# Attention into a token mixer on one core: p read once in fp32, all first scores by 32-row pieces, a new order

## The chip, the cores and the metric

The kernel runs on one core of a Trainium2 chip. The metric is the device time of one execution in microseconds (us), the median of the runs.

## The reference, cut to what matters

Two stages of attention through 32 packed queries p per head, then a token mixer over the joined heads. Inputs and output are float32; B = 8 batches, H = 8 heads, S = 576 tokens, 64 channels per head, 32 rows of p, D = 512.

```python
def sm_attn(qq, kk, vv):
    s = scale * qq @ kk.T                       # per batch and head
    a = exp(s - max(s)); a = a / (sum(a) + 1e-9)
    return a @ vv
p_packed = sm_attn(p, k, v)                     # 32 x 64 per head
x = sm_attn(q, p_packed, p_packed)              # 576 x 64 per head, heads joined: 576 x 512
wq, wk = x @ w_q, x @ w_k                       # 576 x 64
W_tok = scale * wq @ wk.T                       # 576 x 576
out = maximum(W_tok @ x, 0) @ w_out             # 576 x 512
```

## The kernel before, in words

The kernel is a list of named steps, the string ORDER, which a loop at the end of the program walks through once. Each item is a step with its batch, a piece, an engine (`@A` ScalarE, which the profile calls ACT; `@V` VectorE, DVE; `@P` GpSimd, POOL) and, behind `=`, the banks of PSUM that it writes. The order of the items is the order of the instructions on each engine; waits between engines come from the data. So ORDER alone sets what stands ahead of what, on every engine and every DMA queue.

What the steps are, in the order in which one batch b passes through them:

- **LD.x** loads. Loads on GpSimd's queue cast float32 to bf16 on the way: `k`, `q`, `v` a batch each (1.18 MB read; v in two transfers; for batch 0, and q of batch 7, a half at a time under the letters g, q and r), `W` the two small weights, `O` the output weight, `P` a quarter of p. `LD.E0`, `LD.E1` (line 164) read p of batches 0 and 1 in float32 on the ACT and SP queues, `LD.H` (line 171) half of k of batch 0 in float32 on the SP queue. Inputs have four buffers each (NL).
- **EC, EX, PB** cast, transpose and place p of batches 0 and 1 in a block-diagonal form; **HC** casts the half of k; **PX** transposes p of all batches, late, just ahead of batch 2.
- **KT** (line 242, DVE) transposes k; **S1** is p times k. Batches 0 and 1 (DIAG) take 36 matmuls of 128 columns each with the block-diagonal p (line 278); the others take 32 pieces of 32 rows (line 288). **X1** is the exponential (one instruction of 1152 columns for DIAG, line 296; else two halves, line 299), **TE** the transposes that the second way needs.
- **PV** (line 321) is scores times v with the row sums, **RC, PP, PT** normalise, mask and transpose the packed result.
- **QV** transposes q (line 242), **S2** (line 379) is q times the packed result. Its pieces: 0 and 1 are two token blocks of 128 each, 2 the last block, 3 the first four blocks together. **X2** (line 384) is the exponential, **RS** (line 400) the row sums, **RR** (line 405) their reciprocal, **AM** (line 411) the product of both, on DVE or GpSimd. HA halves what RS sums, for batch 5 alone.
- **AT** (lines 420 and 425) transposes the attention on TensorE, **AE** copies it out of PSUM.
- **QK, QKE, QD** multiply the packed result by the small weights; **WKQ, WE** make wk and wq of the tokens; **GM, GE, Y, YE** (lines 473 and 483) contract over the tokens; **MX, MR** (lines 498 and 504) are the mixed tokens, **RL, RLR, RLF** the ReLU; **OT** (line 546) is the product with w_out, four matmuls of 512 columns for each of five row blocks, **OH** (line 583) two halves of the last; **OE, OEF, OEH** (lines 127 and 131, shared with all other copies) copy it to SBUF, and **ST, STF, STH** store it.
- **WARM.n** (line 621) are matmuls of zeros over 128 n columns, written into an idle bank, whose result nobody reads. **HOLD.v7** is a tiny transfer on the SP queue that waits for the last v, so that the stores that stand behind it on that queue go out after the inputs.

Of the kernel before, what the change touches and what calls it, by code (L numbers as in the profile page):

```python
# [654 lines left out]
```

## Time and profile before

| | |
|---|---|
| median of 3 runs | 105.79 us (105.73 to 105.80) |
| the profiled execution | 105.87 us, span 103.7 us |
| PE busy | 97.0 us (94%), of these 24 us by the zeros of line 621 |
| DVE, ACT, POOL busy | 75.7, 66.2 and 49.5 us |
| read and written | 30.28 MB and 9.44 MB |
| last input load issued, first store behind HOLD.v7 issued | 64.7 us, 76.9 us |
| last matmul ends, last store issued | 99.45 us, 99.9 us |

All times in the profile count from the start of the span, whose 103.7 us are 2.2 us less than the execution's own time. PE is TensorE, PEld its weight loads. A PE that is busy is not at its peak: matmuls are pipelined and their ends are modelled. The DMA row gives the mean busy share of the 16 DMA engines, the GB/s row what they wrote; a load that casts writes half of the bytes that it reads.

### The profile page before, as it was taken

How to read it: one execution, taken by the hardware profiler on the slowest of the kernel's cores; microseconds unless marked ns; L12 is line 12 of the kernel's file. 1: busy time of each engine (PE TensorE's matmuls, PEld its weight loads, DVE VectorE, ACT ScalarE, POOL GpSimd, SP SyncE). 2: the span in 40 equal slices, each digit the busy share in tenths (PEclk: the TensorE clock that was granted, in tenths of full speed). 3: DMA queues.
4: the chain of work that ended last, by engine and by line, in shares of the span. 5: the costliest groups of instructions: out<-in, count | busy, mean ns of one | idle time of the engine just before them, and what ended most of it. 6: DMA issues, size and time to landing. Idle time of an engine off the chain costs nothing.

```text
span 103.7 us, 3603 instructions
## 1 busy us (share of the span) xinstructions
PE 97.0 (94%) x1544; PEld 58.6 (57%) x1544; DVE 75.7 (73%) x151; ACT 66.2 (64%) x109; POOL 49.5 (48%) x75
## 2 busy tenths in 40 slices
PE   5999999999999999799999999999999999999930
PEld 3897645666656644456546655683567654744420
DVE  5090382969899799798699979989988998616210
ACT  5243104246896864779869869898997796658430
POOL 5999372952163326920059599405689038000000
PEclk9999999999999999999999999999999999999996
DMA  3999999999999999999999999999999999999883
GB/s 108 238 180 186 202 210 200 211 210 212 209 211 209 206 208 214 212 210 205 213 212 207 216 208 207 215 210 205 210 251 344 396 398 400 402 409 403 330 315 115
DMA packets 14079, 25.16 MB, mean 243 GB/s; under 512 B 2160, under 2 KB 7024, under 8 KB 14064
## 3 DMA queue, kind: packets, MB, share of 16 engines
q0 software_dynamic: 10448, 16.88, 84.7%
q1 hardware_dynamic: 3200, 7.87, 19.9%
q8 instruction: 12, 0.20, 0.7%
q10 hardware_dynamic: 416, 0.20, 0.7%
q14 instruction: 3, 0.02, 0.1%
HBM read 30.28 MB, written 9.44 MB: 383 GB/s over the span
## 4 chain that ended last, share of the span: by engine, by line
PE 81%; DVE 9%; ACT 3%; POOL 2%; issue 1%; DVEq 0%; POOLq 0%; ACTq 0%
PE ps L546 25%; PE ps L621 19%; PE ps L321 6%; PE ps L379 5%; PE ps L452 4%; PE ps L498 3%; PE ps L425 3%; DVE rs L400 3%; PE ps L447 3%; PE ps L473 3%; PE ps L278 2%; PE ps L342 2%; PE ps L288 2%; POOL a L411 2%; DVE a L411 2%; ACT e L384 2%
## 5 line engine op out<-in xcount | busy, mean ns | idle before, releaser
L546 PE MATMUL ps<-wout,relu 128*128 128x512 bf16 x124 | 30.5, 380 | 0.0
L621 PE MATMUL ps<-o 128*128 128x128 f32 (+3 forms) x76 | 23.7, 455 | 1.3 <-DVE o L134 1.2
L411 POOL TENSOR_TENSOR a<-e,rr 128x1024 bf16<-128x1024 f32 (+2 forms) x13 | 15.6, 1212 | 19.1 <-DVE rr L405 10.5
L127 ACT ACTIVATE o<-ps 128x1024 f32<-128x1024 f32 (+2 forms) x17 | 15.0, 888 | 7.0 <-PE ps L546 6.4
L546 PEld LDWEIGHTS <-relu 128*128 128x128 bf16 x124 | 10.7, 98 | 12.4 <-issue 1.8
L621 PEld LDWEIGHTS ps<-o 128*128 128x128 f32 x76 | 12.9, 224 | 7.2 <-issue 4.9
L384 ACT ACTIVATE e<-ps 128x256 f32<-128x256 f32 (+2 forms) x19 | 11.3, 621 | 6.0 <-PE ps L379 5.6
L509 ACT ACTIVATE relu<-ps 128x1024 bf16<-128x1024 f32 (+1 forms) x14 | 12.7, 932 | 2.2 <-PE ps L498 1.1
L176 POOL DMA_DIRECT2D v_sb<-in_v_dram x16 | 10.1, 636 | 7.3 <-DMA q_sb<-in_q_dram 2.1
L242 DVE STREAM_TRANSPOSE kT<-k_sb 128x1152 uint32<-128x1152 uint32 (+1 forms) x9 | 11.0, 1225 | 3.0 <-DMA k_sb<-in_k_dram 3.0
L242 DVE STREAM_TRANSPOSE qT<-q_sb 128x1152 uint32<-128x1152 uint32 (+1 forms) x10 | 11.2, 1121 | 0.4 <-DMA q_sb<-in_q_dram 0.3
L400 DVE TENSOR_REDUCE rs<-e 128x16 f32<-128x512 f32 (+2 forms) x13 | 10.9, 845 | 0.4 <-ACT e L384 0.4
L321 PE MATMUL ps<-v_sb,e 64*64 64x192 bf16 x288 | 7.6, 245 | 0.6 <-DVE o L131 0.6
L299 ACT ACTIVATE e1T<-ps 128x576 bf16<-128x576 f32 x12 | 7.2, 662 | 1.3 <-PE ps L288 1.2
L127 ACT ACTIVATE aT<-ps 128x128 bf16<-128x128 f32 (+2 forms) x11 | 5.3, 506 | 3.5 <-PE ps L425 2.1
L321 PEld LDWEIGHTS <-e 64*64 64x64 bf16 x288 | 6.1, 106 | 2.5 <-issue 0.8
L127 ACT ACTIVATE wkq<-ps 128x448 bf16<-128x448 f32 (+1 forms) x9 | 6.3, 713 | 1.7 <-PE ps L452 1.4
L452 PE MATMUL ps<-aT,pqk 128*128 128x256 bf16 (+1 forms) x48 | 6.8, 246 | 0.1
L379 PEld LDWEIGHTS <-qT 64*128 64x128 bf16 x320 | 5.5, 94 | 2.3 <-issue 0.7
L379 PE MATMUL ps<-ppT,qT 64*128 64x64 bf16 x320 | 6.6, 190 | 0.0
L179 POOL DMA_DIRECT2D k_sb<-in_k_dram x7 | 5.2, 743 | 3.0 <-ACT pqk L127 3.0
L447 PE MATMUL ps<-pqk,aT 128*128 128x64 bf16 x80 | 6.1, 194 | 0.1
(79 smaller groups left out, 142.8 us busy)
## 6 DMA issues: line engine op xcount, KB each, us to landing
v_sb<-in_v_dram POOLq DMA_DIRECT2D x16, 288.0 KB, 11.9
out_dram<-o SPq DMA_DIRECT2D x9, 512.0 KB, 6.9
k_sb<-in_k_dram POOLq DMA_DIRECT2D x7, 576.0 KB, 12.1
q_sb<-in_q_dram POOLq DMA_DIRECT2D x6, 576.0 KB, 15.3
out_dram<-o POOLq DMA_DIRECT2D x4, 512.0 KB, 7.6
out_dram<-o SPq DMA_DIRECT2D x5, 256.0 KB, 3.3
q_sb<-in_q_dram POOLq DMA_DIRECT2D x4, 288.0 KB, 11.1
out_dram<-orem SPq DMA_DIRECT2D x4, 256.0 KB, 5.6
```

The source lines that it names most:

```text
L127: nc.scalar.activation(o, i, COPY)
L176: nc.gpsimd.dma_start(v_bufs[b % NL][halves(i), 0:7:2], src)
L242: nc.vector.transpose(o, i)
L321: nc.tensor.matmul(T["pv", b][halves(cc), i], lhsT, rhs, start=n == 0, stop=n == R - 1, skip_group_check=True)
L379: nc.tensor.matmul(ps[:, y, t - t0, i], lhsT, rhs, start=e == 0, stop=e == 1)
L384: nc.scalar.activation(e2[:, t0:t1].rearrange("a t (i y n) -> a y (t i) n", i=2, y=2), T["s2", b, c].rearrange("a y t i n -> a y (t i) n") ...
L400: nc.vector.tensor_reduce(rs[:, t0 * H:t1 * H], src, axis=AX, op=ADD)
L411: e.tensor_tensor(a2[:, t0:t1].rearrange("a t i (u l) -> a (t i u) l", l=L), e2v(b, c), T["rr", b][:, t0 * H:t1 * H].to_broadcast((P, (t1 ...
L452: nc.tensor.matmul(o, pqk[:, i, Dl:], aT[:, i, c0:c1], start=i == 0, stop=i == 1)
L509: nc.scalar.activation(o, i, RELU)
L546: nc.tensor.matmul(ps, lhsT, wout[:, j, :], start=j == 0, stop=j == NJ - 1)
L621: nc.tensor.matmul(bank(int(bk), [w]), warm[:, 0:P], rhs, start=True, stop=True)
```

## The change

- p of all batches is read once, in float32, in two transfers of 256 KB on the ACT and the SP queue (`LD.N0`, `LD.N1`), as the first loads. ScalarE casts each half (NC) and DVE transposes each half (PX) at the beginning. The steps EC, EX, PB and the six loads of p go.
- The two small weights follow on the same two queues in float32, and GpSimd casts them (WC).
- k of batch 0 comes whole by GpSimd's casting queue: `LD.h0` in place of `LD.H` and HC.
- DIAG is empty: batches 0 and 1 take the 32-row pieces too, with two X1 and two TE each.
- ORDER is new throughout. Of the steps that are in both, 57 change engine: the products AM of batches 0 to 2 that were on DVE go to GpSimd, AM.6.3 goes from GpSimd to DVE, some copies change between ACT and DVE, and the stores on GpSimd's queue are five in place of four. The WARM items have other places and sizes.

The diff of the code; of ORDER, the beginning and the stretches around the last WARM item and around batches 3 and 5 to 6.

```diff
-DIAG = (0,1)
+DIAG = ()
...
-SET.warm@V SET.v0@V SET.pz0@V LD.E0@A SET.tab@A SET.aT1@V LD.H@S LD.P3 LD.E1@S EC@A EX@V PB.0.1@V LD.g0
-HC@A PB.0.3@V PB.0.2@V PB.0.0@V KT.0.0@V KT.0.1@V LD.v0 WARM.4=0 WARM.16.128=0 S1.0=0,1,2 X1.0.0@A WARM.6=3
-PV.0.0=4,5 PV.0.1 RC.0@V LD.q0 LD.P2 LD.r0 LD.W0 SET.mask@P LD.k1 SET.idf@V SET.aT0@V QV.0.1@V PP.0.0@V PP.0.1@V PT.0@V
-SET.v2@V QV.0.0@V WARM.15=3 S2.0.2=6,7 LD.W1 SET.v3@P SET.aT2@V LD.P1 KT.1.2@V S2.0.1=0,1 X2.0.1@A RS.0.1@V
-SET.v1@P S2.0.0=2,3 X2.0.0@A LD.v1 LD.P0 WARM.8=4 QK.0=4 RR.0.1@V AM.0.1@V QKE.0@A LD.q1 RS.0.0@V SET.aff@P
...
-PP.2.0@V AE.1.0@V WARM.2=7 WKQ.1.0=0,1 WKQ.1.2 WARM.2=7 WKQ.1.1 QV.2.2@V WE.1.0@A PT.2@V S2.2.3=4,5 S2.2.2=2,3
-KT.3.2@V WE.1.1@A GM.1=7 QK.2=6 GE.1@V WARM.3=0 Y.1=0,1 X2.2.2@A QKE.2@V S1.3=2,3,6,7 X2.2.3@A RS.2.4@V
-RR.2.4@V LD.v4 X1.3.1@A TE.3.1@V X1.3.0@A TE.3.0@V OT.0.0=4,5 OT.0.1 LD.q4 YE.1@A AM.2.2@V OT.0.2=6,7 OE.0.0@V
-OT.0.3 MR.1=2,3 OE.0.1@A RLR.1@V MX.1.1=0,1 PV.3.0=4,5 PV.3.1 RL.1.1@A RC.3@V PP.3.1@V PP.3.0@V KT.4.2@V
...
-QKE.3@A S2.3.2=4,5 X2.3.2@A S2.3.3=2,3 X2.3.3@A GE.2@V Y.2=0,1 OT.1.1 OE.1.0@A TE.4.0@V YE.2@V PV.4.0=4,5
-PV.4.1 MX.2.0=0,1 RL.2.0@A RS.3.4@V LD.v5 RR.3.4@V RC.4@V LD.q5 PP.4.1@V PP.4.0@V PT.4@V OT.1.2=2,3 OT.1.3
-QK.4=6 QV.4.2@V MX.2.1=0,1 MR.2=4,5 OE.1.1@A RL.2.1@A RLR.2@V AM.3.3@P QKE.4@V AT.3.3=7 AE.3.3@V QD.3@P
...
+LD.N0@A LD.N1@S SET.warm@V SET.aT0@V SET.aT1@V SET.aT2@V SET.idf@V LD.W0@A LD.W1@S SET.tab@A LD.h0 LD.g0 LD.v0
+LD.r0 LD.q0 LD.k1 SET.v0@V NC.1@A PX.1@V NC.0@A PX.0@V SET.aff@P SET.idb@V KT.0.0@V KT.0.1@V SET.mask@P
+WARM.4=0 WARM.22.128=0 S1.0=0,1,2,3 X1.0.1@A TE.0.1@V X1.0.0@A TE.0.0@V SET.v2@P WARM.8=4 PV.0.0=4,5 PV.0.1
+RC.0@V PP.0.0@V PP.0.1@V PT.0@V WC.0@P QV.0.0@V WC.1@P WARM.6=6 QK.0=6 SET.v3@P QV.0.1@V QKE.0@A WARM.4=7
+S2.0.2=2,3 X2.0.2@A RS.0.2@V RR.0.2@V SET.v1@P S2.0.0=0,1 X2.0.0@A LD.v1 LD.q1 LD.k2 S2.0.1=4,5 X2.0.1@A LD.v2
+AM.0.2@P WARM.6=7 AT.0.2=7 AE.0.2@A RS.0.0@V RR.0.0@V KT.1.2@V WARM.5=6 S1.1=2,3,0,1 X1.1.0@A AM.0.0@P
+RS.0.1@V AT.0.0=6 RR.0.1@V AE.0.0@V TE.1.0@V QD.0@P WARM.2=4 WKQ.0.0=4,5 WKQ.0.2 X1.1.1@A TE.1.1@V AM.0.1@P
+AT.0.1=7 LD.q2 PV.1.0=2,3 PV.1.1 WE.0.0@V RC.1@V AE.0.1@A WKQ.0.1 WE.0.1@A WARM.2=6 GM.0=6 LD.k3 PP.1.1@V
...
+LD.k4 RC.2@V PP.2.0@V AT.1.1=6 AE.1.1@A LD.q3 LD.v4 WKQ.1.0=4,5 WKQ.1.2 WE.1.0@A PP.2.1@V WKQ.1.1 WE.1.1@A
+PT.2@V QK.2=2 QKE.2@A QV.2.2@V LD.q4 WARM.1=3 GM.1=3 QD.2@P GE.1@A WARM.1=7 Y.1=6,7 S2.2.2=0,1 X2.2.2@A
+KT.3.2@V S2.2.3=4,5 YE.1@A WARM.1=2 MX.1.0=2,3 X2.2.3@A MX.1.1=0,1 MR.1=6,7 RLR.1@A RS.2.4@V RL.1.0@A RR.2.4@V
+S1.3=4,5,6,7 X1.3.1@A X1.3.0@A TE.3.1@V OT.1.4=2 OT.0.2=6,7 OEF.1.4@A RL.1.1@V AM.2.2@P AT.2.2=3 AE.2.2@V
+AM.2.3@P OT.0.3 OT.0.0=4,5 AT.2.3=2 TE.3.0@V PV.3.0=0,1 PV.3.1 OE.0.1@V LD.k5 OT.0.1 RC.3@V PP.3.1@V PP.3.0@V
...
+S2.3.2=2,3 X2.3.2@A S2.3.3=4,5 MX.2.1=6,7 MX.2.0=2,3 OT.1.2=0,1 TE.4.1@V X2.3.3@A QD.3@P OT.1.3 RS.3.4@V
+MR.2=4,5 RR.3.4@V AM.3.3@P AM.3.2@P RL.2.1@A RLR.2@V LD.v6 PV.4.0=6,7 RL.2.0@A PV.4.1 LD.q6 RC.4@V PP.4.1@V
+OE.1.1@A PP.4.0@V PT.4@V OT.2.2=2,3 QK.4=4 QV.4.2@V AT.3.3=5 QKE.4@A AT.3.2=4 AE.3.2@A S2.4.2=0,1 X2.4.2@A
...
+TE.6.1@V OT.3.4=2 OEF.3.4@V GM.4=3 GE.4@A S2.5.2=0,1 ST.0.0@P X2.5.2@A S2.5.3=4,5 X2.5.3@A Y.4=6,7 YE.4@V
+PV.6.0=0,1 PV.6.1 MR.4=2,3 RC.6@V PP.6.1@V PP.6.0@V PT.6@V ST.1.4 MX.4.0=6,7 RLR.4@A ST.0.1 MX.4.1=4,5
+OT.3.2=2,3 OT.3.3 QV.6.2@V RL.4.0@A RL.4.1@A OE.3.1@A QK.5=1 QKE.5@A QK.6=0 QKE.6@A HA.5@P RS.5.4@V RR.5.4@V
+S2.6.2=6,7 X2.6.2@A KT.7.2@V ST.1.1@P S2.6.3=4,5 X2.6.3@A RS.6.4@V OT.4.0=2,3 OT.4.1 S1.7=0,1,6,7 OE.4.0@A
+AM.5.3@P AM.5.2@P AT.5.3=4 AT.5.2=5 AE.5.3@A OT.4.2=2,3 X1.7.1@A AE.5.2@V QD.5@P X1.7.0@A ST.2.0 WKQ.5.0=4,5
+WKQ.5.1 WKQ.5.2 OT.4.3 WE.5.2@A RR.6.4@V AM.6.3@V AT.6.3=6 QV.7.1@V GM.5=7 AM.6.2@P TE.7.0@V AT.6.2=0 OE.4.1@A
...
-        elif a == "P":
-            c = int(b)
-            src = p.rearrange("b (i c) (y l) d -> c (b i) y (l d)", i=2, y=2)
-            nc.gpsimd.dma_start(pbf[quarter(c)], src[c])
-        elif a == "E":
-            b = int(b)
-            src = p[b].rearrange("(i c) l d -> (c l) i d", i=2)
-            (nc.sync if eng == "S" else nc.scalar).dma_start(p32[:, 2 * b:2 * b + 2], src)
+        elif a == "N":
+            i, n = int(b), L * Dh // 4
+            src = p.rearrange("b (i c) (z l) d -> i (c z) b (l d)", i=2, z=4)
+            (nc.sync if eng == "S" else nc.scalar).dma_start(p32[:, i * n:(i + 1) * n], src[i])
         elif a == "W":
             w = (moe_w_k, moe_w_q)[int(b)].rearrange("(i c j e) m -> (c j) i (e m)", i=2, c=4, e=2)
-            nc.gpsimd.dma_start(wqk[:, :, int(b)].rearrange("a i e m -> a i (e m)"), w)
+            (nc.sync if eng == "S" else nc.scalar).dma_start(w32[:, int(b)], w)
...
-        elif a == "H":
-            nc.sync.dma_start(h32, pairs(k, 0)[:, 0])
+        elif a == "h":
+            nc.gpsimd.dma_start(k_in[0][:, 0], pairs(k, 0)[:, 0])
...
-    def EC(eng, bk):
-        copy(eng, pbe, p32.rearrange("a u d -> a (u d)"))
-
-    def HC(eng, bk):
-        copy(eng, k_in[0][:, 0], h32)
-
-    def EX(eng, bk):
-        blocks(pe.rearrange("a u l e -> a (u l e)").bitcast(u32), pbe.bitcast(u32))
-
-    def PX(eng, bk):
-        blocks(pT.rearrange("a u (y l) e -> a (u y l e)", y=2).bitcast(u32).rearrange("a (u l) -> a l u", l=L // 2),
-               pbf.bitcast(u32).rearrange("a (l n) -> a l n", l=L // 2))
+    def NC(x, eng, bk):
+        n = L * Dh // 4
+        copy(eng, pbf[:, x * n:(x + 1) * n], p32[:, x * n:(x + 1) * n])
+
+    def WC(x, eng, bk):
+        copy(eng, wqk[:, :, x].rearrange("a i e m -> a i (e m)"), w32[:, x])
+
+    def PX(x, eng, bk):
+        blocks(pT.rearrange("a u l e -> a (u l e)").bitcast(u32)
+               .rearrange("a (b i z l) -> a i l z b", b=B, i=2, z=4)[:, x],
+               pbf.bitcast(u32).rearrange("a (i l z b) -> a i l z b", i=2, b=B, z=4)[:, x])
```

More of the change, by code (lines that the diff above doesn't have):

```diff
@@ new lines @@
+RS.0.1@V AT.0.0=6 RR.0.1@V AE.0.0@V TE.1.0@V QD.0@P WARM.2=4 WKQ.0.0=4,5 WKQ.0.2 X1.1.1@A TE.1.1@V AM.0.1@P
+AT.0.1=7 LD.q2 PV.1.0=2,3 PV.1.1 WE.0.0@V RC.1@V AE.0.1@A WKQ.0.1 WE.0.1@A WARM.2=6 GM.0=6 LD.k3 PP.1.1@V
+PP.1.0@V PT.1@V QV.1.2@V GE.0@A WARM.1=0 Y.0=0,1 YE.0@A QK.1=4 QKE.1@V WARM.1=7 S2.1.2=2,3 S2.1.1=6,7 X2.1.2@A
+RS.1.2@V S2.1.0=0,1 X2.1.1@A LD.O MR.0=4,5 RR.1.2@V AM.1.2@P RLR.0@A KT.2.2@V MX.0.1=2,3 WARM.3=6 AT.1.2=6
+X2.1.0@A QD.1@P WARM.1=7 S1.2=4,5,0,1 RL.0.1@A LD.v3 AE.1.2@A MX.0.0=2,3 X1.2.1@A RS.1.0@V RR.1.0@V RS.1.1@V
@@ new lines @@
+AM.1.0@P X1.2.0@A TE.2.1@V RR.1.1@V AM.1.1@P TE.2.0@V RL.0.0@A WARM.6=7 AT.1.0=7 AE.1.0@V PV.2.0=0,1 PV.2.1
+LD.k4 RC.2@V PP.2.0@V AT.1.1=6 AE.1.1@A LD.q3 LD.v4 WKQ.1.0=4,5 WKQ.1.2 WE.1.0@A PP.2.1@V WKQ.1.1 WE.1.1@A
+PT.2@V QK.2=2 QKE.2@A QV.2.2@V LD.q4 WARM.1=3 GM.1=3 QD.2@P GE.1@A WARM.1=7 Y.1=6,7 S2.2.2=0,1 X2.2.2@A
+KT.3.2@V S2.2.3=4,5 YE.1@A WARM.1=2 MX.1.0=2,3 X2.2.3@A MX.1.1=0,1 MR.1=6,7 RLR.1@A RS.2.4@V RL.1.0@A RR.2.4@V
+S1.3=4,5,6,7 X1.3.1@A X1.3.0@A TE.3.1@V OT.1.4=2 OT.0.2=6,7 OEF.1.4@A RL.1.1@V AM.2.2@P AT.2.2=3 AE.2.2@V
@@ L56 @@
+OT.7.4=4 RLF.7.0.0@V RLF.7.1.0@A RLF.7.0.1@V OT.7.2=0 OEF.7.2@V OEF.6.3@A ST.6.0 STF.6.3 OT.7.0=5 OEF.7.0@V
+OEF.7.4@A ST.7.4 OT.7.1=1 OH.7.1=0 OEH.7.1@V STF.7.2 OH.7.0=7 OEH.7.0@V STF.7.0 OEF.7.1@A STF.7.1 STH.7.1@A
+STH.7.0
 """
@@ L596, in STF @@
         q.dma_start(orows(b)[:, :, t * D:(t + 1) * D], T["o", b][:, t])
-    steps = dict(EC=EC, HC=HC, EX=EX, PX=PX, PB=PB, KT=KT, S1=S1, X1=X1, TE=TE, PV=PV, RC=RC, PP=PP,
+    steps = dict(NC=NC, WC=WC, PX=PX, PB=PB, KT=KT, S1=S1, X1=X1, TE=TE, PV=PV, RC=RC, PP=PP,
                  PT=PT, QK=QK, QKE=QKE, QD=QD, QV=QV, S2=S2, X2=X2, HA=HA, RS=RS, RR=RR, AM=AM,
```

54 lines of the change are left out of this document (18 added, 36 removed).

## The prediction

> **What bounds the kernel now.** I read the page first, then the busy time by stretches, then the chain that ended last in order of time, then the timeline at the places where that chain leaves TensorE.
>
> ```profile
> span 103.7 us, 3603 instructions
> ...
> PE 97.0 (94%) x1544; PEld 58.6 (57%) x1544; DVE 75.7 (73%) x151; ACT 66.2 (64%) x109; POOL 49.5 (48%) x75
> ...
> PE   5999999999999999799999999999999999999930
> ...
> DMA  3999999999999999999999999999999999999883
> GB/s 108 238 180 186 202 210 200 211 210 212 209 211 209 206 208 214 212 210 205 213 212 207 216 208 207 215 210 205 210 251 344 396 398 400 402 409 403 330 315 115
> ...
> q1 hardware_dynamic: 3200, 7.87, 19.9%
> ...
> q10 hardware_dynamic: 416, 0.20, 0.7%
> ...
> HBM read 30.28 MB, written 9.44 MB: 383 GB/s over the span
> ...
> PE 81%; DVE 9%; ACT 3%; POOL 2%; issue 1%; DVEq 0%; POOLq 0%; ACTq 0%
> PE ps L546 25%; PE ps L621 19%; PE ps L321 6%; PE ps L379 5%; PE ps L452 4%; PE ps L498 3%; PE ps L425 3%; DVE rs L400 3%; PE ps L447 3%; PE ps L473 3%; PE ps L278 2%; PE ps L342 2%; PE ps L288 2%; POOL a L411 2%; DVE a L411 2%; ACT e L384
> ```
>
> The page shows two things that are full at once. PE is busy for nine tenths or more of nearly every slice, and 81% of the chain is PE. The DMA row is as full: nines from the second slice on. The GB/s row has two levels, some 210 while the casting queue reads (it counts what is written; bf16 is half of the fp32 that is read) and some 400 while stores run.
>
> ```profile
> 2.00:77.00 75.00, 73.69 (x1260) 45.26 (x1259) 59.92 (x118) 49.37 (x81) 41.84 (x63) 1.00 1.14 211
> 77.00:102.00 25.00, 22.45 (x285) 12.83 (x283) 14.76 (x32) 16.12 (x29) 6.80 (x9) 1.00 0.96 370
> ...
> 76.00:78.00 2.00, 2.00 (x30) 1.48 (x27) 1.56 (x4) 1.65 (x5) 1.69 (x2) 1.00 0.77 236
> ...
> 100.00:102.00 2.00, 0.00 (x0) 0.00 (x0) 0.00 (x0) 0.00 (x0) 0.00 (x0) 0.98 0.90 322
> ```
>
> The first row is the inputs, the second the stores. The inputs take the DMA engines whole for 75 us. In 76 to 78 the share falls to 0.77: inputs have ended and the held stores have hardly begun.
>
> PE's own fullness deceives: the WARM matmuls of zeros (L621) are 19% of the chain. So I looked for the last of them.
>
> ```profile
> 35.45 0.78 PE L379 MATMUL ps<-ppT,qT 64*128 64x64 bf16 x40
> ...
> 35.83 1.38 DVE L242 STREAM_TRANSPOSE kT<-k_sb 128x1152 uint32<-128x1152 uint32 x1 [0.55 <-DMA k_sb<-in_k_dram]
> ...
> 36.90 0.91 PE L621 MATMUL ps<-o 128*128 128x384 f32 x2
> ...
> 37.75 0.25 PE L483 MATMUL ps<-pp,g 64*64 64x128 bf16 x4
> ...
> 39.70 1.90 POOL L411 TENSOR_TENSOR a<-e,rr 128x1024 bf16<-128x1024 f32 x1 [2.90 <-DVE rr L405]
> 40.16 1.73 DVE L411 TENSOR_TENSOR a<-e,rr 128x256 bf16<-128x256 f32 x1
> ...
> 43.07 0.94 PE L321 MATMUL ps<-v_sb,e 64*64 64x192 bf16 x36 [0.62 <-DVE o L131]
> ```
>
> The last filler ends where Y.1 begins, at 37.75. From there to the end of PE's work every matmul is real. The only gap before the one at 54.9 is 0.62 us before PV.3 at 43.07, where PE waited for a bank that DVE was emptying.
>
> ```profile
> PE ps L425 <- POOL a L411: 0.3, 1, 0.3
> ```
> ```profile
> 48.76 0.89 PE ps L379 x40
> ...
> 49.73 1.03 ACT e L384
> 50.79 1.50 DVE rs L400
> ...
> 52.38 0.40 DVE rr L405
> ...
> 52.94 1.91 POOL a L411
> ...
> 54.90 0.62 PE ps L425 x8
> ...
> 58.04 0.41 PE ps L288 x22
> ...
> 60.79 0.81 PE ps L321 x36
> 61.60 0.54 PE ps L498 x4
> ...
> 69.78 0.22 PE ps L342 x8
> ...
> 72.60 0.06 PE ps L504 x4
> ...
> 73.14 1.88 PE ps L546 x8
> ...
> 98.58 0.89 PE ps L583 x8
> 99.49 0.39 ACT o L127
> ```
>
> The second gap, 0.3 us, is before AT.3.3 at 54.90: the softmax chain of batch 3 (ACT 1.03, DVE sum 1.50, reciprocal 0.40, GpSimd product 1.91) is 5.25 us from the end of S2.3 at 49.65 to AT.3.3, and PE has a little less work than that. After 54.90 the chain is PE alone until 98.58 + 0.89 = 99.47. So three things bound this kernel in turn: the arrival of inputs until about 36 us, PE with two small gaps until 99.47, and then a fixed tail of 103.7 - 99.47 = 4.2 us (the last copy, its store, the end of the program). The stores would take over if PE were much quicker: in 100 to 102 the DMA share is still 0.90.
>
> **The change, part by part.** *The input stream.* The p of batches 0 and 1 is no longer read twice: 2 x 65.5 KB = 0.131 MB of 30.28 MB. At the inputs' rate (211 GB/s written, 422 read) that is 0.31 us. Those loads have rows of 256 bytes. The ACT queue (q10) held one of them and the last store, and took 0.7% of 103.7 = 0.73 us of all engines for 0.20 MB; q1 took 19.9% = 20.6 us for 7.87 MB, or 0.382 MB/us. The last store's 0.131 MB is then 0.34 us, which leaves 0.38 us for one such load, 0.77 for both. So the stream ends 0.3 to 0.8 us sooner; I take 0.5. The other bytes only change queue: p, weights and half of k. The Trainium skill (DMA: Bandwidth & Descriptors, section "Issuing engines are not separate DMA queues") says that this saves issue time and no transfer time; by it alone the gain would be the 0.31 us of bytes. No row here separates the two.
>
> *The first batch.* Removed: the two ACT copies EC and HC, one small DVE transpose, four DVE copies, one memset and the late PX. Added: two ACT casts (NC), two half PX, two GpSimd casts (WC), and for batches 0 and 1 two exponentials and two transposes (X1, TE) in place of one exponential each. All of it lies before 20 us, where PE has WARM in plenty. I cost it at nothing; its cover is that WARM and the wait for k1. If that cover is gone, S1.0 waits for the second half of k: 0.27 MB more stands before k1's end in the queues (p and weights 0.786, the three tensors of batch 0 3.54, k1 1.18: 5.51 MB; before, with half of p, one weight and E, 5.24), 0.27/0.422 = 0.65 us. I keep 0 to 0.65; by k2 the order has levelled out, because the P loads and weights then lie ahead of it in both.
>
> *The last filler.* This is the largest term. Before, S2.2 starts at 35.45 and behind it come GM.1, QK.2 and WARM.3, because Y.1 needs the copy of GM.1: real work starts at 37.75. In the new order GM.1, QK.2 and Y.1 stand before S2.2, behind it only 128 columns of filler, a third of the 0.85 us of WARM.3. So the last filler ends at 35.45 - 0.5 (stream) + 0.71 (S2.2) + 0.3 = 36.0, 1.75 us sooner. S1.3 soon after needs k3: its transpose at 35.83 moves to 35.3 and ends at 36.7, when PE has just done the three small steps before (36.0 + 0.54 for two MX + 0.06 for MR). What PE has yet to do is the same list as before less Y.1 (0.2 us). Before, 99.47 - 37.75 = 61.7 held 0.9 us of gaps. So with no gaps PE would end at 36.0 + 61.7 - 0.9 - 0.2 = 96.6, 2.85 us sooner.
>
> *New gaps.* The products AM of batches 0 to 2 go from DVE to GpSimd.
>
> ```profile
> L411 POOL TENSOR_TENSOR a<-e,rr 128x256 bf16<-128x256 f32 x5 | 3.1, 620 | 1.4 <-DVE rr L405 1.3
> ...
> L411 DVE TENSOR_TENSOR a<-e,rr 128x512 bf16<-128x512 f32 x3 | 2.1, 687 | 0.1
> ...
> L490 ACT ACTIVATE y<-ps 128x256 bf16<-128x256 f32 x4 | 1.5, 387 | 0.0
> ```
>
> At AT.2.2 the chain from the end of S2.2.3 is YE.1 0.39 (ACT, ahead of it), exponential 1.03, sum 1.47 to 1.50, reciprocal 0.40, product on GpSimd 0.62, and 0.25 us of hops as in the chain above: 4.2 us. PE has filler 0.3, two MX 0.54, MR 0.06, S1.3 0.41, OT.1.4 and OT.0.2 at 0.94 each: 3.2. Gap 1.0. At AT.2.3 the second product takes 1.9 behind the first, beside two OT of 1.88: 0.1. At AT.3.3 the chain is the measured 5.25, and PE has two MX 0.54, OT.1.2, OT.1.3 and OT.2.2 2.82, PV.4 0.81, QK.4 and MR.2 0.28: 4.45. Gap 0.8. At AT.3.2 the next product is 0.62 against AT.3.3's 0.55 to 0.62: 0.1 with its hop. For batches 4 to 6 I summed PE's list between the end of S2 and the first AT in the same way: 5.9, 6.9 and 5.4 us. The chains are 5.25 + 0.62 = 5.9 (batch 4, both products first), at most 5.25 + 1.91 - 0.75 = 6.4 (batch 5, where GpSimd first halves what DVE sums), and 1.03 + 1.50 + 0.40 + 1.37 (AM.6.3 on DVE, two of 0.69) + 0.5 = 4.8 (batch 6). So no gap there. Sum 2.0 to 2.1 us. Net for PE: 2.85 - 2.1 = 0.75 us sooner. The bounds of this difference: 2.85 with no gap at all, and a loss where each gap grows by 0.5.
>
> One row speaks about these products. DVE's product of 128x256 took 1.73 us at 40.16 while GpSimd's product ran from 39.70 to 41.60; the 128x512 form, twice the size, takes 0.69 alone. The new order puts AM.2.2 on GpSimd too, ahead of AM.2.3, so that this collision goes, and puts AM.6.3 on DVE beside AM.6.2 on GpSimd, so that one can come. The Trainium skill (SBUF — State Buffer, "SBUF: two separate sides") says that the two engines share a port pair as an exclusive lock for an instruction's whole length; by it AM.6.3 would wait out the GpSimd product; the trace agrees so far, as DVE's product ended 0.29 us after GpSimd's. In rows such a wait is 0.62 us (AM.6.2), which the 0.6 by which PE's 5.4 exceeds 4.8 just covers. I count nothing for it.
>
> *The stores and the tail.* Two stores instead of one now stand on GpSimd's queue before AM.5.3, so the 0.23 x 2 = 0.46 us hole of 76 to 78 should fill. With the stream's 0.5 that gives the DMA side up to 1.0 us, more than PE's 0.75, so PE still sets the end. The last copy goes from ACT (0.39) to DVE: nothing.
>
> Sum against the profiled execution: 105.87 - 0.75 = 105.12. The median of the three runs shown is 0.08 lower, so about 105.1.
>
> **Rivals.** *Faster still.* The gaps at AT.2.2 and AT.3.3 are smaller than worked out, since DVE and ACT also run 0.5 us sooner there. For it: the stores have 1.0 us of room. Against: they have no more. 1.0 to 1.6 us less, about 104.5.
>
> *No change.* The stream's gain is lost in the start (0.65 against 0.5), and the gaps take the rest: 105.8.
>
> *Slower: the product chain takes the lead.* DVE is busy 75.7 us, from 30 to 90 us nearly without pause, and its queue is in order. At AT.2.2, AT.3.3, AT.4.2 and AT.6.3 the sum, the reciprocal and copies share it, and GpSimd gives the products one by one at 1.91 per 128x1024. If every one of these four comes 0.5 us later than summed, the gaps are 2.1 + 2.0 = 4.1, over 2.85 by 1.25; if two do, over by 0.25. It decides from 2.85 us of gaps. I put it at 106.6. For it: both gaps of before end on exactly these engines. Against: OT steps can be late only where PE has nothing else, and the later batches have margin.
>
> *Slower: the casting queue runs dry.* The loads of q2 and k3 stand behind AM.0.1 on GpSimd, those of v3 and k4 behind AM.1.2 and AM.1.1. Up to v2 the queues hold 0.786 + 3.54 + five tensors of 1.18 = 10.2 MB, 24 us at 0.422 MB/us, so till about 26, and a load takes some us from issue to first data: q2 should be issued by 23 or 24.
>
> ```profile
> 19.82 0.69 DVE L411 TENSOR_TENSOR a<-e,rr 128x512 bf16<-128x512 f32 x1
> ```
>
> AM.0.1 began at 19.82 on DVE before. Now a second sum and reciprocal (0.9) stand ahead of it, and it takes 1.0 itself on GpSimd (half of 1.90): done by 22. It decides from 24 on; each us late costs one, so done by 25.4 would make 105.1 + 1.4 = 106.5.
>
> **How the numbers follow.** Differences within 0.2% (0.2 us) can't be told from none. Forecast 0.40, faster still 0.12: faster 0.52. No change 0.09. Product chain 0.30, queue dry 0.09: slower 0.39. The forecast's own range is 104.7 to 105.5. The range 104.2 to 106.8 takes in the rival below for the most part and both above up to their worked prices; what lies outside is a loss at four places of more than 0.5 us each, and a gain beyond 1.6.
>
> **What would show it.** Right: the last L621 matmul ends near 36, PE waits for L411 once near 40 and once near 50 with 2 us in sum, k3's transpose starts near 35.3, PE ends near 98.7, DMA share in 76 to 78 above 0.9. Wrong: PE waits for L411 or for DVE above 3 us after the last filler, in more than two batches; a DMA share under 1.0 before 70 us; or PE's end sooner with the tail longer than 4.2 us, which would mean that the stores set the end.

## The result, and the profile after

The changed kernel takes 111.22 us (median of 4, 110.19 to 111.99), the kernel before, run beside it, 105.76 us: a ratio of 1.0494, 95% interval 1.0402 to 1.0586. The forecast was 105.1 us, range 104.2 to 106.8. It missed by 6.1 us, on the other side of the kernel before. An execution more than 1.5% above the fastest of its kernel is left out of all ratios and differences: 111.99 here (the other three have a median of 110.82 us), 109.28 in e11 (107.08) and 111.98 in e12 (110.15).

The profiled execution took 110.82 us. From its page, the rows that answer to those of before:

```profile
span 109.0 us, 3595 instructions
...
PE 95.1 (87%) x1531; PEld 57.8 (53%) x1546; DVE 73.2 (67%) x139; ACT 65.2 (60%) x112; POOL 53.2 (49%) x83
...
PE   5993079999999998899997989999999999999950
...
PEclk9999655999999999999999999999999999999997
DMA  2999999999599999999999999999999998954895
GB/s 27 262 230 210 212 209 206 218 208 203 64 172 213 187 205 190 209 205 219 207 207 211 213 212 206 203 199 208 172 316 414 403 415 343 369 213 192 328 362 176
...
PE 63%; DVE 10%; DMA 8%; ACT 7%; POOL 5%; issue 3%; DVEq 0%; POOLq 0%; ACTq 0%
```

Three slices of PE (3 to 5, counted from 0, some 8 to 16 us) hold 3, 0 and 7 tenths, where before had nines. The granted clock falls to 6 and 5 tenths in slices 4 to 6. The share of PE in the chain fell from 81% to 63%. One holder is new in it, DMA with 8%, and ACT and POOL have grown from 3% and 2% to 7% and 5%; DVE has 10% where it had 9%. The chain that ended last, in order of time, near its beginning (start, length, what):

```profile
3.16 8.49 DMA v_sb<-in_v_dram
...
11.90 0.54 DVE v_sb L206
...
13.44 1.31 DVE kT L237 x2
...
14.79 0.70 PE ps L282 x23
15.50 3.50 PE ps L615 x4
```

The first 11.6 us hang on the load of v of batch 0, and what ends that wait is a memset (L206, of v's buffer) on DVE. Behind it stand the transposes of k, then the first scores (L282), then filler. DVE's timeline (start, length, form; in brackets the idle time before, with what ended it) and one row of ScalarE's:

```profile
11.90 0.54 DVE L206 MEMSET v_sb<- 128x576 uint32 x1 [10.38 <-DMA v_sb<-in_v_dram]
12.35 1.03 DVE L237 STREAM_TRANSPOSE pT<-o 128x256 uint32<-128x256 uint32 x2
...
13.35 0.74 DVE L237 STREAM_TRANSPOSE kT<-k_sb 128x576 uint32<-128x576 uint32 x1
```

```profile
5.49 1.15 ACT L128 ACTIVATE o<-o 128x512 bf16<-128x512 f32 x2 [1.93 <-DMA o<-in_p_dram]
```

ScalarE had cast p by 6.64, so the transposes of p could have begun there; they began at 12.35. DVE did nothing for 10.38 us. The reason is in the order: the memset `SET.v0@V`, which fills the columns of ones beside v in buffer 0, stands behind `LD.v0` in the new ORDER. The load has been issued into that buffer, so the memset waits until it has landed, and everything behind it on DVE waits too. Before, the same memset was the second thing that DVE did, ahead of the load:

```profile
1.21 0.54 DVE L209 MEMSET v_sb<- 128x576 uint32 x1
```

The Trainium skill (TensorE: Matmul & The Clock Gate, section "Architectural detail: the array is 16× 32×32, not 1× 128×128") calls the queues of ScalarE and VectorE strict first-in, first-out; the 10.38 us with ready work behind the memset agree.

The stretches of the changed kernel (from:to, length, busy time and count on PE, PEld, DVE, ACT, POOL, granted clock, DMA share, GB/s):

```profile
9.00:14.00 5.00, 0.06 (x1) 0.10 (x1) 2.10 (x5) 0.00 (x0) 4.39 (x8) 0.78 1.16 210
14.00:20.00 6.00, 5.63 (x73) 2.41 (x73) 1.75 (x5) 1.19 (x2) 1.00 (x2) 0.61 1.16 209
28.00:30.00 2.00, 1.92 (x52) 1.49 (x51) 1.34 (x5) 0.68 (x2) 2.00 (x4) 1.00 0.43 40
```

From 9 to 14 PE does nothing, from 14 to 20 the clock averages 0.61. From 28 to 30 the DMA share is 0.43: the loads behind AM.0.1, which ends at 28.2, were issued late, and the queue ran empty. That is the rival of the dry casting queue in plain sight, so it needed an experiment. And MX.1, behind the last filler, and TensorE's last matmuls:

```profile
42.52 0.61 PE L492 MATMUL ps<-wkq,y 64*128 64x512 bf16 x4
...
104.15 1.04 PE L577 MATMUL ps<-wout,relu 128*128 128x256 bf16 x8
```

The last filler ends where MX.1 starts, at 42.52, against a forecast of 36.0. PE ends at 105.2, against 98.7.

### The profile page after: what moved, and what is told of

Same layout as the page of the kernel before. It is cut to its first block, busy times and chain, and to the rows that moved or that the text cites. A ratio compares the mean times of both kernels' runs of the same rounds, so it can differ in the third digit from the quotient of the medians.

```text
span 109.0 us, 3595 instructions
## 1 busy us (share of the span) xinstructions
PE 95.1 (87%) x1531; PEld 57.8 (53%) x1546; DVE 73.2 (67%) x139; ACT 65.2 (60%) x112; POOL 53.2 (49%) x83
## 4 chain that ended last, share of the span: by engine, by line
PE 63%; DVE 10%; DMA 8%; ACT 7%; POOL 5%; issue 3%; DVEq 0%; POOLq 0%; ACTq 0%
PE ps L540 26%; PE ps L615 8%; DMA v_sb<-in_v_dram 8%; PE ps L315 6%; PE ps L419 4%; PE ps L373 4%; DVE kT L237 4%; ACT e L378 3%; POOL a L405 3%; DVE rs L394 3%; PE ps L446 3%; PE ps L282 3%; PE ps L467 2%; PE ps L492 2%; PE ps L441 2%
## 5 line engine op out<-in xcount | busy, mean ns | idle before, releaser
L405 POOL TENSOR_TENSOR a<-e,rr 128x256 bf16<-128x256 f32 (+2 forms) x18 | 19.6, 1098 | 31.9 <-DVE rr L399 24.6
L540 PE MATMUL ps<-wout,relu 128*128 128x512 bf16 x112 | 29.2, 380 | 1.0 <-issue 0.5
L615 PEld LDWEIGHTS ps<-o 128*128 128x128 f32 x86 | 13.5, 216 | 6.8 <-issue 4.6
L293 ACT ACTIVATE e1T<-ps 128x576 bf16<-128x576 f32 x16 | 9.7, 655 | 11.5 <-PE ps L282 11.5
L128 ACT ACTIVATE o<-ps 128x1024 f32<-128x1024 f32 (+1 forms) x13 | 12.5, 959 | 4.2 <-PE ps L540 3.9
L503 ACT ACTIVATE relu<-ps 128x1024 bf16<-128x1024 f32 (+1 forms) x12 | 11.2, 957 | 1.3 <-PE ps L492 1.2
L282 PE MATMUL ps<-kT,pT 32*32 32x288 bf16 x256 | 4.8, 307 | 5.8 <-DVE kT L237 5.6
L128 ACT ACTIVATE aT<-ps 128x128 bf16<-128x128 f32 (+2 forms) x12 | 6.4, 548 | 5.8 <-PE ps L419 4.4
L237 DVE STREAM_TRANSPOSE e<-e1T 128x288 uint32<-128x288 uint32 x16 | 7.1, 458 | 1.8 <-ACT e1T L293 1.5
L132 DVE COPY o<-ps 128x512 f32<-128x512 f32 (+2 forms) x7 | 5.4, 768 | 3.4 <-PE ps L540 2.7
L206 DVE MEMSET v_sb<- 128x576 uint32 x1 | 0.5, 538 | 10.4 <-DMA v_sb<-in_v_dram 10.4
```

Source lines behind the costliest of these rows:

```text
L128: nc.scalar.activation(o, i, COPY)
L237: nc.vector.transpose(o, i)
L293: nc.scalar.activation(e1T[:, x], T["s1", b][x].rearrange("a c m -> a m c"), EXP, scale=scale)
L405: e.tensor_tensor(a2[:, t0:t1].rearrange("a t i (u l) -> a (t i u) l", l=L), e2v(b, c), T["rr", b][:, t0 * H:t1 * H].to_broadcast((P, (t1 ...
L503: nc.scalar.activation(o, i, RELU)
L540: nc.tensor.matmul(ps, lhsT, wout[:, j, :], start=j == 0, stop=j == NJ - 1)
```

## The experiments

The theory after this reading: the place of one memset costs the whole loss, some 5 us because the first batch begins late and 1 to 2 us because TensorE's clock has fallen by then (the array has "cooled"). Rivals: the empty casting queue at 28 to 30; the new loads themselves; the new order of the later batches. "e1" below is the changed kernel with the memset put back.

### 1. The memset ahead of the load, and in two other places

e1, on the changed kernel:

```diff
-LD.N0@A LD.N1@S SET.warm@V SET.aT0@V SET.aT1@V ... LD.h0 LD.g0 LD.v0
+LD.N0@A LD.N1@S SET.warm@V SET.v0@V SET.aT0@V SET.aT1@V ... LD.h0 LD.g0 LD.v0
-LD.r0 LD.q0 LD.k1 SET.v0@V NC.1@A PX.1@V
+LD.r0 LD.q0 LD.k1 NC.1@A PX.1@V
```

> The changed kernel with one item moved: SET.v0@V (the ones beside v of batch 0) stands ahead of LD.v0 again, as before the change. In the changed kernel DVE waits 10.4 us in this memset for the load of v0, and both halves of PX and KT.0 stand behind it. Theory A (this wait starts the whole loss, the rest follows from it): S1.0 starts near 9 instead of 14.1, the casting queue does not run dry near 28, and the time falls to 104.5 to 106. Theory B (the start has slack, the loss is made by the products on GpSimd and the new order): 109 or more, with the gaps after 36 us in place. Theory C (half of each): 107 to 108.

Measured: 104.47 us (104.01 to 104.74), ratio 0.9886 [0.9846, 0.9927] to the kernel before. One word moved is worth 110.82 - 104.47 = 6.35 us, and the change is then a gain of 1.1%. TensorE's timeline of e1, at the start and at the last filler:

```profile
9.48 0.47 PE L282 MATMUL ps<-kT,pT 32*32 32x288 bf16 x30 [0.24 <-DVE kT L237]
9.88 1.98 PE L615 MATMUL ps<-o 128*128 128x512 f32 x4
```

```profile
36.00 0.61 PE L492 MATMUL ps<-wkq,y 64*128 64x512 bf16 x4
```

S1.0 (its main group of 30 matmuls) starts 14.79 - 9.48 = 5.31 us sooner, MX.1 6.52 us sooner, and the last filler ends at 36.00: the figure of the forecast.

e2 leaves the memset behind the load, but puts it behind the transposes of k:

```diff
-LD.r0 LD.q0 LD.k1 SET.v0@V NC.1@A PX.1@V NC.0@A PX.0@V SET.aff@P SET.idb@V KT.0.0@V KT.0.1@V SET.mask@P
+LD.r0 LD.q0 LD.k1 NC.1@A PX.1@V NC.0@A PX.0@V SET.aff@P SET.idb@V KT.0.0@V KT.0.1@V SET.v0@V SET.mask@P
```

> The changed kernel with SET.v0@V moved behind KT.0 on DVE, still behind LD.v0: the wait stays, but only TE.0 and what follows stand behind it. Theory A in its exact form (it costs what stands behind it): S1.0 near 9, the transposes of batch 0's scores near 12.5, PV.0 near 13.5 instead of 19, time 105 to 106.5. If the wait itself were the cost wherever it stands: 109 to 111.

Measured: 105.13 us (104.90 to 105.22, 9 runs), ratio 0.9947 [0.9931, 0.9964]. Rows of e2's timeline:

```profile
9.53 0.47 PE L282 MATMUL ps<-kT,pT 32*32 32x288 bf16 x30 [0.58 <-DVE kT L237]
...
11.79 0.54 DVE L206 MEMSET v_sb<- 128x576 uint32 x1 [2.31 <-DMA v_sb<-in_v_dram]
...
13.07 0.94 PE L315 MATMUL ps<-v_sb,e 64*64 64x192 bf16 x36 [1.16 <-DVE e L237]
```

The memset still waits for the load (2.31 us), but ahead of it S1.0 has gone out at 9.53 as in e1. What is left behind it are the transposes of the exponentials: PV.0 starts at 13.07, where e1 has it at 11.81. Of these 1.26 us, 0.66 us reach the time; the transpose of k of batch 1, for which DVE waits in e1 (0.46 us, at 18.27), starts at 18.99 without a wait, and MX.1 at 36.67, 0.67 us after e1's. So it is what stands behind the wait that costs, and not the wait.

e4 puts the fault into the kernel before:

```diff
-SET.warm@V SET.v0@V SET.pz0@V LD.E0@A ... PB.0.1@V LD.g0
-HC@A PB.0.3@V ... KT.0.0@V KT.0.1@V LD.v0 WARM.4=0
+SET.warm@V SET.pz0@V LD.E0@A ... PB.0.1@V LD.g0 LD.v0 SET.v0@V
+HC@A PB.0.3@V ... KT.0.0@V KT.0.1@V WARM.4=0
```

> The kernel before with the same fault put in: SET.v0@V moved behind LD.v0, ahead of the last three PB copies and KT.0. Theory A: DVE waits for v0 until about 9.5, S1.0 starts near 12 instead of 8.3, and PE idles with its clock falling; but here no product on GpSimd stands ahead of the loads of q2 and k3, so the casting queue should not run dry: 107 to 109. Theory B (slack): within 0.3 us of 105.8.

Measured: 113.12 us (112.71 to 113.53), ratio 1.071 [1.0666, 1.0753]. Of e4's timeline:

```profile
11.15 0.54 DVE L209 MEMSET v_sb<- 128x576 uint32 x1 [4.92 <-DMA v_sb<-in_v_dram]
...
13.95 2.13 PE L278 MATMUL ps<-o,kT 128*64 128x128 bf16 x35 [0.34 <-DVE kT L242]
```

The old order, with none of the new loads, loses 113.12 - 105.55 = 7.6 us from the same misplacement. Here the first scores start at 13.29 in place of 8.29, at half clock. That is more than the 107 to 109 us expected; why it exceeds the loss of the changed kernel is left open. The fault belongs to neither order.

### 2. What the cold array costs

e3 keeps the fault and lengthens the filler ahead of S1.0, so that PE does not stand still while DVE waits:

```diff
-WARM.4=0 WARM.22.128=0 S1.0=0,1,2,3
+WARM.4=0 WARM.42.128=0 S1.0=0,1,2,3
```

> The changed kernel with the filler ahead of S1.0 lengthened from 22 to 42 pieces of 128 columns, so that PE works through DVE's wait; the wait itself stays. In the changed kernel PE stands idle from 9 to 14 and its granted clock reads 0.5 from about 11.5 to 18.5; four filler matmuls there took 3.5 us. Theory A: the wait stays, so at most the 1.7 to 2 us of slow filler ahead of PV.0 come back: 108.5 to 110. Rival (the fallen clock is the loss): below 107.

Measured: 109.68 us (109.44 to 109.94), ratio 1.0386 [1.0342, 1.0429]. TensorE of e3:

```profile
14.85 0.47 PE L282 MATMUL ps<-kT,pT 32*32 32x288 bf16 x30 [0.36 <-DVE kT L237]
```

```profile
40.78 0.61 PE L492 MATMUL ps<-wkq,y 64*128 64x512 bf16 x4
```

S1.0 starts as late as before the edit, at 14.85, but its 30 matmuls take 0.47 us in place of 0.70, and the mean granted clock is 1.00 in place of 0.96. From S1.0 to MX.1 are 25.9 us, in the changed kernel 42.52 - 14.79 = 27.7. 110.82 - 109.68 = 1.1 us is therefore the price of the cooling (1.7 between e5 and e6 below, which differ in the same way); 109.68 - 104.47 = 5.2 us is the price of the delay, for a start 14.85 - 9.48 = 5.37 us later. The traces show where the first price is paid: the four filler matmuls behind S1.0 take 3.50 us in the changed kernel and 1.98 in e1.

e10 and e11 take the 15 WARM items behind S1.0 out (6144 columns of zeros, no part of the result), from e3 and from e1:

```diff
-TE.0.0@V SET.v2@P WARM.8=4 PV.0.0=4,5 PV.0.1
+TE.0.0@V SET.v2@P PV.0.0=4,5 PV.0.1
...
```

> e3_long_warm (late memset kept, clock kept up until S1.0) without the 15 WARM items behind S1.0, 6144 columns that took some 14 us of PE between S1.0 and MX.1. From S1.0 to MX.1.0 PE took 26.5 us in e1_memset_first, 25.9 in e3 and 27.7 in the changed kernel, though in the last two the data of batches 1 and 2 had landed long before. Theory E (filler runs in full even when the data are there, so PE's program can't catch up): S1.0 to MX.1 shortens by 2 to 4 us, time 106 to 108. Rival F (the softmax and copy chains of batches 0 to 2 on ACT, DVE and GpSimd are what takes 26 us): within 0.5 of 109.7, or slower if PE's clock falls in the gaps.

> e1_memset_first without the 15 WARM items behind S1.0. If they fill only time in which PE has nothing else: within 0.3 of e1 (104.5). If the granted clock falls without them (it read 0.5 after 2.5 us without matmuls in the changed kernel): slower, 105 to 107. If they hold real work back in e1 too: 103 to 104.2.

Measured: e10 112.26 us (111.34 to 112.31), ratio 1.061 [1.0565, 1.0655]; e11 107.38 us (106.86 to 109.28), ratio 1.0152 [1.011, 1.0194]. Both are slower with less work, by 112.26 - 109.68 = 2.6 and 107.08 - 104.47 = 2.6 us. TensorE of e10, and its longest waits from 15 to 44 us (sum, times, longest):

```profile
14.93 0.47 PE L282 MATMUL ps<-kT,pT 32*32 32x288 bf16 x30 [0.36 <-DVE kT L237]
...
43.24 0.61 PE L492 MATMUL ps<-wkq,y 64*128 64x512 bf16 x4 [0.33 <-ACT y L484]
```

```profile
PE ps L414 <- POOL a L405: 2.2, 2, 1.1
PE ps L315 <- DVE e L237: 1.9, 1, 1.9
```

Without filler the stretch from S1.0 to MX.1 takes 43.24 - 14.93 = 28.3 us, not less than the 40.78 - 14.85 = 25.9 of e3. PE waits in it for GpSimd's products and DVE's transposes instead. But the clock falls in both runs, which lengthens TensorE's own work too, so they do not measure the filler alone. Up to the first scores of batch 1 (S1.1) e11 can be read:

```profile
19.96 0.71 PE L282 MATMUL ps<-kT,pT 32*32 32x288 bf16 x32 [1.13 <-DVE kT L237]
```

With no filler ahead of it, S1.1 starts 0.26 us later than in e1 (19.70), not sooner, and PE waits 1.13 us for DVE there. Up to that point the filler of e1 holds nothing back. For the rest of the stretch this is argued and not shown: the chain of e3 goes through 7.1 us of filler (6.6% of 107.9). At half clock the filler did hold work back: in the changed kernel the exponentials of batch 0 are transposed by 17.29 and PV.0 starts at 18.93, behind the slow filler; in e3 it starts at 17.18. What is shown is that at full clock the stretch from S1.0 to MX.1 has one length of about 26 us (25.9 in e3; 26.5 in e1, of which DVE waits 0.46 for k of batch 1) and moves with its beginning. And the filler holds the clock:

```profile
14.00:20.00 6.00, 2.39 (x61) 1.68 (x62) 5.09 (x11) 2.13 (x5) 2.88 (x5) 0.50 1.16 209
```

In e11 the clock is 0.50 in this stretch.

### 3. The empty casting queue

e5, on the changed kernel, issues three loads ahead of the product that they stood behind; e6 adds the longer filler of e3:

```diff
-AM.0.2@P WARM.6=7 AT.0.2=7
+LD.q2 LD.k3 LD.O AM.0.2@P WARM.6=7 AT.0.2=7
...
-AT.0.1=7 LD.q2 PV.1.0=2,3
+AT.0.1=7 PV.1.0=2,3
...
```

> The changed kernel, its late memset kept, with the loads of q2, k3 and the output weight issued on GpSimd ahead of the products of batch 0 instead of behind them. In the changed kernel GpSimd waits for those products until 28.2 and the DMA share falls to 0.43 in 28 to 30 (with parts of 26 to 32 some 2.5 us of stream are lost). Theory A2 (of the 5.5 us lost, the dry casting queue is the second half): the hole goes, the last inputs land some 2.5 us sooner, 108 to 109.5. Rival (the late start alone carries the loss; PE is behind anyway): the hole goes and the time stays within 0.5 us of 111.

> As e5_loads_early, and with the long filler of e3_long_warm that keeps PE's clock up through DVE's wait. What is left against e1_memset_first is then the plain delay of the first batch. If the parts add up (clock 1.5, hole up to 2.5): 106.5 to 108. If PE's delay is the whole and the hole costs nothing by itself: as e3, 109.7.

Measured: e5 111.30 us (110.89 to 111.80), ratio 1.0513 [1.0446, 1.0579]; e6 109.61 us (109.31 to 110.75), ratio 1.0374 [1.0307, 1.044]. Neither differs clearly from its counterpart (110.82 with a spread of 110.19 to 111.62, and 109.68). The stretch of e5:

```profile
28.00:30.00 2.00, 1.90 (x51) 1.44 (x50) 1.60 (x4) 1.30 (x3) 0.83 (x1) 1.00 1.13 217
```

The DMA share there is 1.13 in place of 0.43, and nothing is gained. The queue did run dry, and it cost nothing that can be told from the spread. That the work which needed those loads was itself 5 us late would explain it; this was not tested. With the first batch in time, in e1, AM.0.1 ends at 21.70 and the DMA share stays above 1.1 from 20 to 30.

### 4. The new loads alone

e7 has the code, the loads and the 32-row pieces of the change, and the order of the kernel before for all the rest.

> The loads, casts and 32-row pieces of the changed kernel in the order of the kernel before: p by two hardware transfers, weights behind, k0 by the casting queue, no block-diagonal batches; from batch 1's softmax on every step, engine and filler as before, SET.v0@V first. It parts the 1.1 us by which e1_memset_first beats the kernel before. If the loads carry it (the stream ends 0.3 to 0.8 us sooner): 105.0 to 105.3. If the new order carries it: within 0.2 us of the kernel before.

Measured: 106.49 us (106.25 to 107.59, 12 runs), ratio 1.0078 [1.0042, 1.0114]. DVE and TensorE of e7 (its lines count one lower than those of the changed kernel), beside DVE of the kernel before:

```profile
18.75 1.38 DVE L236 STREAM_TRANSPOSE kT<-k_sb 128x1152 uint32<-128x1152 uint32 x1 [2.79 <-DMA k_sb<-in_k_dram]
```

```profile
39.16 0.25 PE L476 MATMUL ps<-pp,g 64*64 64x128 bf16 x4
```

```profile
17.56 1.38 DVE L242 STREAM_TRANSPOSE kT<-k_sb 128x1152 uint32<-128x1152 uint32 x1 [2.17 <-DMA k_sb<-in_k_dram]
```

Neither case of the expectation held: the new loads and pieces by themselves cost 106.49 - 105.59 = 0.9 us. In the profiled execution k of batch 1 lands 1.19 us later and the last filler ends 39.16 - 37.75 = 1.41 us later; that execution took 107.59 us, one of the two longest of the twelve, so these two may be larger than in the others. The new order with the memset in place (e1) is 106.49 - 104.47 = 2.0 us faster than e7. So the gain comes from the order, and the loads take some of it back.

e12 tries to have that back: e1 with the weights loaded behind the first exponential and used later, so that k of batch 1 comes ahead of them.

```diff
-SET.idf@V LD.W0@A LD.W1@S SET.tab@A LD.h0
+SET.idf@V SET.tab@A LD.h0
-X1.0.0@A TE.0.0@V
+X1.0.0@A LD.W0@A LD.W1@A TE.0.0@V
-PT.0@V WC.0@P QV.0.0@V WC.1@P WARM.6=6 QK.0=6 SET.v3@P QV.0.1@V QKE.0@A WARM.4=7
+PT.0@V QV.0.0@V WARM.6=6 SET.v3@P QV.0.1@V WARM.4=7
-S2.0.1=4,5 X2.0.1@A LD.v2
+S2.0.1=4,5 X2.0.1@A LD.v2 WC.0@P WC.1@P QK.0=6 QKE.0@A
```

> The changed kernel with the memset of buffer 0 ahead of its load (104.47 us so far), and in it the two weight loads moved from their place ahead of k1 to ScalarE's queue behind the first exponential, with their products and the copies of the weights behind the first batch's second scores. The whole computation is done. There k1 landed at 18.25 us and its transpose waited for it; the weights are 0.262 MB, 0.6 us at the stream's rate. Theory G (k1's landing sets the early chain, and what goes ahead of it in the stream is paid in full): the first transpose of k1 starts 0.4 to 0.6 us sooner, near 17.7, and the time is 103.8 to 104.3 us. Rival H (the end is set by k7's landing and the last batches' products, whatever the early chain does): k1's transpose is sooner, and the time stays within 0.2 us of 104.47. If the weights' products come too late for the bridge that uses them, TensorE shows a new wait and the time is above 104.8.

Measured: 110.22 us (109.86 to 111.98, 7 runs), ratio 1.0437 [1.0416, 1.0457]. The last case of the expectation came true, with a price far above what I had in mind. Rows of e12:

```profile
17.72 1.38 DVE L237 STREAM_TRANSPOSE kT<-k_sb 128x1152 uint32<-128x1152 uint32 x1 [0.35 <-DMA k_sb<-in_k_dram]
18.02 0.40 POOL L130 CAST wqk<-o 128x256 bf16<-128x256 f32 x1 [4.95 <-DMA o<-in_moe_w_k_dram]
...
20.13 1.62 POOL L405 TENSOR_TENSOR a<-e,rr 128x256 bf16<-128x256 f32 x2
20.21 0.63 PE L336 MATMUL ps<-wqk,ppT 64*64 64x128 bf16 x8 [4.31 <-POOL wqk L130]
```

```profile
15.18 0.72 PE L373 MATMUL ps<-ppT,qT 64*128 64x64 bf16 x36 [0.19 <-DVE qT L237]
...
20.77 2.93 PE L615 MATMUL ps<-o 128*128 128x512 f32 x4
...
25.99 0.48 PE L282 MATMUL ps<-kT,pT 32*32 32x288 bf16 x32
...
42.27 0.61 PE L492 MATMUL ps<-wkq,y 64*128 64x512 bf16 x4
```

```profile
20.00:26.00 6.00, 5.79 (x21) 3.00 (x20) 0.00 (x0) 0.66 (x2) 5.20 (x8) 0.51 1.12 210
```

The transpose of k of batch 1 does start 0.55 us sooner (17.72 against 18.27), as theory G had it. But the weights land only at 18.0 and 19.8. GpSimd waits for them 4.95 and 1.34 us with the products AM behind them on its queue (20.13, against 17.13 in e1), and TensorE stands still 4.31 us ahead of QK.0. Then the clock is 0.51 from 20 to 26, the filler takes 2.93 us, S1.1 starts at 25.99 in place of 19.70, and MX.1 at 42.27 in place of 36.00: 6.3 us later, 110.15 - 104.47 = 5.7 us in the time. I had made the same mistake again, on another engine, at nearly the same cost. Whether the 0.55 us is worth anything is left open.

### 5. The end of the kernel

e8 is e1 with the store ST.1.1 on GpSimd's queue moved from ahead of AM.5.3 to ahead of ST.3.1, so that one store less goes out early; e9 is e1 with S1.7, which waited for the last k, behind AT.5.3.

```diff
-KT.7.2@V ST.1.1@P S2.6.3=4,5
+KT.7.2@V S2.6.3=4,5
...
-ST.3.1@P PP.7.0@V
+ST.1.1@P ST.3.1@P PP.7.0@V
```

> e1_memset_first with the second early store on GpSimd's queue (ST.1.1) issued behind the products of batches 5 and 6 again, so that one store instead of two stands behind the last loads. The DMA share in 75 to 77 (1.09 and 1.03 in e1) should fall below 0.9. If the stores set the end: 0.4 us slower than e1. If PE does (in e1 the share falls to 0.57 at 92 and 0.16 at 94, so the stores wait for results there): within 0.2 us of e1.

Measured: 104.60 us (104.03 to 104.94), ratio 0.9915 [0.9885, 0.9945], as e1. The hole that I expected to come back in 76 to 78 did not (DMA share 1.02), so this run doesn't price it; but neither does the place of that store matter.

```diff
-OT.4.1 S1.7=0,1,6,7 OE.4.0@A
+OT.4.1 OE.4.0@A
-AM.5.3@P AM.5.2@P AT.5.3=4 AT.5.2=5
+AM.5.3@P AM.5.2@P AT.5.3=4 S1.7=0,1,6,7 AT.5.2=5
```

> e1_memset_first with S1.7 moved behind AT.5.3 on PE. In e1 PE stands idle for 0.4 us at 74.2 until k of batch 7 has landed and is transposed, while the product for AT.5.3 is ready at 74.35. Theory D (in e1 this arrival is one of the gaps that set PE's end, the stores have room): 104.1 to 104.3. Rival (the scores of batch 7 come later by as much and the gap moves on): 104.5 to 105.

Measured: 104.68 us (104.26 to 105.10), ratio 0.9888 [0.9845, 0.9931], as e1. PE's waits for k from 36 to 100 us are 0.3 us in place of the 0.7 of e1 (shown below), and the time does not follow. The chain of e1 goes through this load (k of batch 7, 11.62 us from issue to landing, ahead of its transpose at 73.17), that of e9 no longer, and nothing is gained; why is left open. No version is measurably faster than e1.

## Why the prediction was wrong

**The step that failed** is the first batch: "All of it lies before 20 us, where PE has WARM in plenty. I cost it at nothing; its cover is that WARM and the wait for k1." Two things were wrong in it.

First, the step listed what the change adds and removes, and costed the new order only from the casting queue's loads near 20 us on. Of the beginning it counted instructions, but didn't walk DVE's queue through. `SET.v0@V` is in both orders, so it was on no list of added steps; it had only been moved past a load into its own buffer. The line with it was printed in the diff above.

Second, the cover does not exist. WARM fills PE's waiting, but PE is not what is late there: without filler S1.1 is no sooner (19.96 in e11, 19.70 in e1), because PE then waits for DVE. A delay ahead of S1.0 goes through to the end nearly one for one (5.37 us late in e3, 5.2 us in the time). The other cover named, the wait for k of batch 1, hides only a little: in e2, 1.26 us at PV.0 had become 0.72 at that transpose. Because PE's busy time there is zeros, it was read as slack; a chain that waits on other engines has none.

**The sum of the loss**: 5.2 us delay (e3 against e1) and 1.1 us of fallen clock (changed kernel against e3). They add up to the 6.35 us by construction, as e3 stands between the two. What supports them is the traces: a first batch 5.3 us late, and filler that takes 1.5 us longer. The empty queue adds nothing that can be told (e5, e6).

**The other terms**, in e1, where the memset is out of the way:
- *The last filler* was forecast to end at 36.0 and ended at 36.00.
- *The gaps of PE behind it* were forecast at 2.1 us. The waits of e1's PE from 36 to 100 us (sum, times, longest) come to the same 2.1 us:

```profile
PE ps L282 <- DVE kT L237: 0.7, 2, 0.4
PE ps L540 <- ACT relu L503: 0.4, 1, 0.4
PE ps L336 <- DVE ppT L237: 0.4, 1, 0.4
PE ps L282 <- ACT e L378: 0.2, 1, 0.2
PE ps L419 <- POOL a L405: 0.2, 1, 0.2
PE ps L441 <- ACT aT L128: 0.2, 1, 0.2
```

But they lie elsewhere. At AT.2.2, where I had 1.0 us, PE had already waited for the exponential (0.2) and the ReLU (0.4) ahead of it; at AT.3.3 it is 0.2 for the product (forecast 0.8) behind 0.4 for a transpose; two waits for k (0.7) were not foreseen. That the sums agree is partly luck.
- *PE's end and the tail*: 98.7 and 4.2 us forecast.

```profile
98.06 1.04 PE L577 MATMUL ps<-wout,relu 128*128 128x256 bf16 x8
```

PE ends at 99.10, 0.4 us later, and the 102.9 us of the span leave a tail of 3.8 us, 0.4 us shorter. The profiled execution of e1 is 104.74 us where the sum said 105.12.
- *The stream and the first batch's bound*: the stream gain of 0.5 us (0.3 to 0.8) doesn't show at the beginning, but it does at the end: the tiny transfer of HOLD.v7, which waits for the last v, goes out at 76.25 before, at 75.40 in e1 and at 75.16 in e7, 0.85 and 1.1 us sooner. The late k was bounded at 0 to 0.65 us and measured at 0.71 in e1 (18.27 against 17.56) and 1.19 in e7's long execution. The bound counted bytes alone.
- *The hole of 76 to 78* filled, but in e7 already, with the stores in their old order, so it did not need the two early stores; no gain could be laid to it.

```profile
76.00:78.00 2.00, 2.00 (x51) 1.03 (x49) 1.97 (x3) 2.00 (x4) 2.00 (x3) 1.00 1.01 339
```

- *AM.6.3 beside AM.6.2*, costed at nothing, shows among no wait of PE above. The two products do collide in e1, but it is GpSimd's that is held: AM.6.3 runs on DVE from 76.46 to 77.69, and AM.6.2 takes 1.59 us from 76.57, where this form takes 0.62 alone.

**The rivals**: the casting queue did run dry (AM.0.1 done at 28.2, the condition was 24), but its price of 1 us for each us was not paid here; without the late memset (e1) AM.0.1 ends at 21.70, as forecast (by 22), and there is no hole. I had named a DMA share under 1.0 before 70 us as a sign that the prediction was wrong; it was there, as a consequence of the late first batch and not as the cause. The product chain never took the lead: PE waits 0.2 us for products. No rival said that the first batch itself could begin late by more than the 0.65 us of bytes.
